# Tile 0's statistics shared between VectorE and ScalarE, first loads reordered, tile 2 normalised before its transposes, z sum moved to step 8

## The chip, the cores and the metric

The kernel runs on one core of one Trainium2 chip. The metric is the device time of one execution in microseconds. The kernel before took a median of 212.5 us in three runs (212.2, 212.5 and 212.92).

## What is computed

One input `x` (2048 rows of 512 columns, bf16) is normalised per row, and the result `xn` goes through two branches whose outputs are added to `x`:

```python
xn  = layernorm(x)                                   # mean and variance over 512, eps 1e-5
q, k, v = split(xn @ wqkv)                           # 32 heads of 16
pq, pk = phi(q), phi(k)                              # phi(t) = (t+1 if t>0 else exp(t)) + 1e-6
kv, z  = sum_s pk * v, sum_s pk                      # per head, over all rows
A = ((pq @ kv) / (pq . z + 1e-6)) @ wo               # linear attention
B = (silu(xn @ w_gate) * (xn @ w_up)) @ w_down       # 1792 wide
out = x + A + B
```

The outputs are in bf16.

## The kernel before, in words

The rows are cut into 16 tiles of 128. Everything stays in SBUF. The order of work on each engine is written out by hand: a small recorder (`K.op`, `K.dma`) appends each operation to the list of its engine and derives the semaphore waits from the named resources that it reads and writes. So each engine, and each of the two DMA queues (SP's and ACT's), works in exactly the order of the calls.

The program has three stages.

*Start (tiles 0 to 2).* TensorE runs filler matmuls on constants while the first tile of `x` is loaded. VectorE computes a tile's statistics (`bns` at line 291, `agg` at 294), then centres the tile without scaling it (`xc_half`, line 344, two halves of 256 columns). TensorE transposes the halves (`tp_first`, line 356), ScalarE copies them out of PSUM (line 365), and TensorE multiplies them with the key and query weights (`proj_first`, line 395). The row scale `rstd` is applied later, as the per-partition scale of the activations `first_ek`, `first_pk`, `first_eq`, `first_pq` (lines 452 to 470). `rstd_pow` (lines 312 and 319) computes `(var + eps)^-0.5` with an add (on VectorE for the tiles listed in `VD`, on POOL for the others) and a power on POOL.

*Steps (tiles 3 to 15).* VectorE writes the normalised tile `xn` (line 299), a DMA transpose on SP's queue writes `xnT` (line 372), TensorE computes keys and queries (`kproj`, `qproj`, line 381), ScalarE takes exponentials and a copy (lines 418 to 428), VectorE forms the features `pk` (`clip` at 435, `maxadd` at 444), and TensorE adds the outer product of `xn` and `pk` into four PSUM banks (`gtacc`, line 515: G = xn^T pk, from which `kv` is made later by one product with the value weights). POOL sums `pk` over the tiles into `zacc` (`zsum`, lines 503 and 507). One step is eight projection matmuls and four of `gtacc`. Tile t's projections use PSUM banks 2(t%2) and 2(t%2)+1; banks 4 to 7 hold `gtacc`'s sums, and earlier the start's transposes.

In the lists, step t computes the projections of tile t, while `STAT` names the tiles whose statistics are made in that step and `XN0`, `XN` those that are normalised and sent to the DMA transpose. Tiles 0 to 2 are transposed again by DMA (`transpose_dma` in steps 7 to 9), since their normalised form is needed by the last stage.

*Feed-forward stage.* From about 48 us, TensorE runs gate and up projections for 4 chunks of 512 rows x 14 column blocks (`ffn_mm`, line 679), and the output products of a finished chunk (lines 851 and 862) in between. Beside it, `z_split`, `z_cols`, `z_sum` and `z_rows` turn `zacc` into a row sum on every partition (two POOL copies, DMA transposes, a reduce on VectorE at line 734), and the queries' features are divided by their denominators (lines 809 to 833).

The weights are loaded over both queues: keys (`wk`, four chunks of 128 rows) and queries (`wq`) at the start, interleaved with tiles of `x`; the rest on SP's queue in step 10 and at the start of the last stage.

Of the kernel before, what the change touches and what calls it, by code (L numbers as in the profile page):

```python
# [7 lines left out]
ALU = mybir.AluOpType  # L8
# [100 lines left out]
def bass_parallel_sum__linear_attn_block__swiglu_ffn__prompt_kernel(  # L109
# [16 lines left out]
    with contextlib.ExitStack() as es:  # L126
        E = es.enter_context

        def sb(name, shape, d=bf):
            return E(nc.sbuf_tensor(name, [P] + shape, d))  # L130
# [19 lines left out]
        nb = sb("nb", [NT], f32)  # L150
# [44 lines left out]
        def xload(eng, h, t0, n, after=()):  # L195
            K.dma(
                eng, lambda: h.dma_start(x_sb[:, t0:t0 + n, :], xv[:, t0:t0 + n, :]),
                r=list(after), w=[("x", t0 + i) for i in range(n)],
            )
# [40 lines left out]
        xload("sp", sp, 0, 1)  # L240
        wqkv_load("act", act, "wk", 1, 0, 2)
        xload("sp", sp, 1, 1)
        wqkv_load("sp", sp, "wk", 1, 2, 1)
        wqkv_load("act", act, "wk", 1, 3, 1)
        xload("act", act, 2, 1)
        wqkv_load("sp", sp, "wq", 0, 0, 1)
        wqkv_load("act", act, "wq", 0, 1, 1)
        xload("sp", sp, 3, 1)
        wqkv_load("act", act, "wq", 0, 2, 1)
        wqkv_load("sp", sp, "wq", 0, 3, 1)  # L250
        xload("act", act, 5, 1)
        xload("sp", sp, 4, 1)
        xload("sp", sp, 6, 4, [("x", 3)])
# [52 lines left out]
        VD = (3, 5)  # L306
# [34 lines left out]
        def xc_half(t, h):  # L341
            K.op(
                "dve",
                lambda: dve.tensor_scalar(  # L344
                    out=xc_sb[:, t, h * HD:(h + 1) * HD], in0=x_sb[:, t, h * HD:(h + 1) * HD],
                    scalar1=mv[:, t, 0:1], scalar2=None, op0=ALU.subtract,
                ),
                r=[("x", t), ("mv", t)], w=[("xc", t, h)],
            )

        def tp_first(t, h, b):
# [11 lines left out]
            K.op(  # L363
                "act",
                lambda: act.activation(xcT[:, NDC * t + 2 * h:NDC * t + 2 * h + 2, :], tb, ACT.Copy),  # L365
                r=[bk(b)], w=[("xcT", t, h)],
            )
# [120 lines left out]
        def feat_k(t):  # L488
            e = t % NE
            clip(ek[:, e, :], ("ek", e))  # L490
            if t >= 3:
                zsum(t - 3, e)
            maxadd(pkq[:, t, 0, :], banks[kb(t)], ek[:, e, :], [bk(kb(t)), ("ek", e)], [("pk", t)])

# [29 lines left out]
        def stat(t):  # L524
            bns(t)
            agg(t)
            rstd_pow(t)

# [5 lines left out]
        bns(0)  # L534
        agg(0)
        rstd_pow(0)
        xc_half(0, 0)
        xc_half(0, 1)
        bns(1)
        agg(1)  # L540
        rstd_pow(1)
        xc_half(1, 0)
        xc_half(1, 1)
        bns(2)
        agg(2)
        rstd_pow(2)
        xn_dve(0)
        xc_half(2, 0)
        xc_half(2, 1)

        fill(8, 512)
        tp_first(0, 0, 4)
        fill(2, P)
        tp_first(0, 1, 5)
        fill(3, P)
        proj_first(0, "wk", 0)
        proj_first(0, "wk", 1)
        tp_first(1, 0, 6)
        tp_first(1, 1, 7)
        fill(4, P)  # L560
        first_ek(0)
        first_pk(0)
# [5 lines left out]
        tp_first(2, 0, 4)  # L568
        tp_first(2, 1, 5)
        proj_first(0, "wq", 1)  # L570
        proj_first(1, "wq", 1)
        clip(ek[:, 0, :], ("ek", 0))
        feat_pool(0)
        bns(3)
        agg(3)
        rstd_pow(3)
        bns(4)
        clip(ek[:, 1, :], ("ek", 1))
        first_pk(1)
        first_eq(0)  # L580
        first_pq(0)
        proj_first(2, "wk", 0)
        proj_first(2, "wk", 1)
        gtacc(0)
        xn_dve(2)
        xn(3)
        agg(4)
        first_feat(1)
        rstd_pow(4)
        xn_dve(1)  # L590
        first_ek(2)
        first_pk(2)
        first_eq(1)
        first_pq(1)
        clip(ek[:, 2, :], ("ek", 2))
        xn(4)
        proj_first(2, "wq", 0)
        proj_first(2, "wq", 1)
        gtacc(1)
        first_eq(2)  # L600
        xload("act", act, 14, 2)
        first_pq(2)
        first_feat(2)
        bns(5)
        agg(5)
        rstd_pow(5)
        gtacc(2)
        bns(6)
        agg(6)
        rstd_pow(6)  # L610
        xn(5)
        kproj(3)
        exp_k(3)
        qproj(3)
        exp_q(3)
        bns(7)
        clip(ek[:, 0, :], ("ek", 0))
        xn(6)
        agg(7)
        rstd_pow(7)  # L620
        zsum(0, 0)
        maxadd(pkq[:, 3, 0, :], banks[kb(3)], ek[:, 0, :], [bk(kb(3)), ("ek", 0)], [("pk", 3)])
        bns(8)
        xn(7)
        agg(8)
        rstd_pow(8)

        STAT = {4: (9,), 5: (10,), 6: (11,), 7: (12,), 8: (13, 14), 9: (15,)}
        XN0 = {5: (8,), 6: (9,), 7: (10,), 8: (11,), 9: (12, 13), 10: (14,)}
        XN1 = {}  # L630
        XN = {10: (15,)}

        for t in range(4, NT):
# [4 lines left out]
            for i in XN0.get(t, ()):  # L638
                xn(i)
            feat_k(t)  # L640
            for i in XN1.get(t, ()):
                xn(i)
            for i in STAT.get(t, ()):
                stat(i)
            for i in XN.get(t, ()):
                xn(i)
            if t in (7, 8, 9):
                transpose_dma(t - 7)
# [6 lines left out]
            if t == 12:  # L655
                masks()
# [4 lines left out]
        zsum(NT - 3, None)  # L661
        zsum(NT - 2, None)
        zsum(NT - 1, None)
# [236 lines left out]
        whalf("wu", wu_sb, B_w_up, 1)  # L900
# [58 lines left out]
```

## Time and profile before

| | |
|---|---|
| median of three runs | 212.5 us |
| profiled execution | 212.67 us, its span 211.3 us |
| TensorE matmul busy | 208.2 us (98%) |
| VectorE busy | 119.8 us (57%) |
| ScalarE busy | 69.9 us (33%) |
| POOL busy | 74.4 us (35%) |
| moved by DMA | 16.71 MB, mean 79 GB/s |
| granted TensorE clock, mean | 1.0 |

The span runs from the first to the last instruction of the profiled execution; the device time has 1.4 us around it. PE is TensorE, PEld its weight loads, DVE is VectorE, ACT is ScalarE, SP the engine that issues most DMAs. All times of single instructions below are microseconds from the span's start. A matmul on 512 columns is listed with some 0.38 us, because its record includes the pipeline's latency; what counts for throughput is the distance between two starts.

### The profile page before, as it was taken

The page shows a single profiled execution, that of the slowest core. Times are in us where ns is not written, and L with a number is a line of the kernel's source. Part 1 is how long each engine was busy: PE and PEld are TensorE (multiplying, and loading weights), DVE is VectorE, ACT ScalarE, POOL GpSimd, SP SyncE. Part 2 cuts the span into 40 slices and gives each one's busy share as a digit, 9 for nine tenths or more (in the row PEclk, how much of TensorE's full clock was granted, in tenths as well). Part 3 has the DMA queues.
Part 4 walks back from the last instruction along what each step waited for, and adds up shares of the span by engine and source line. Part 5 has one row for each costly group of instructions (what it writes and reads, how often), then busy time and mean ns, then how long its engine had stood idle before and what let it go on. Part 6 is the DMA issues. An engine that isn't in the chain of part 4 may idle for free.

```text
span 211.3 us, 2784 instructions
## 1 busy us (share of the span) xinstructions
PE 208.2 (98%) x995; PEld 96.3 (46%) x995; DVE 119.8 (57%) x245; ACT 69.9 (33%) x122; POOL 74.4 (35%) x95
## 2 busy tenths in 40 slices
PE   8999999999999999999999999999999999999996
PEld 3544444445444444444444444444444444444454
DVE  3899889434464775546274746364556535374121
ACT  3797666766543331213122312212032213121000
POOL 3637987749032444122140432130414032221100
DMA  5863344795694011110101010202021010110201
GB/s 187 281 177 75 54 99 88 197 374 190 165 363 96 0 25 25 50 28 25 50 2 50 19 33 26 50 0 50 3 50 25 25 25 29 48 28 25 51 28 50
DMA packets 29455, 16.71 MB, mean 79 GB/s; under 512 B 20224, under 2 KB 29056, under 8 KB 29440
## 3 DMA queue, kind: packets, MB, share of 16 engines
q1 hardware_dynamic: 28304, 15.34, 26.8%
q10 hardware_dynamic: 1136, 1.18, 1.8%
q8 instruction: 8, 0.13, 0.3%
q14 instruction: 7, 0.06, 0.1%
HBM read 9.70 MB, written 2.10 MB: 56 GB/s over the span
## 4 chain that ended last, share of the span: by engine, by line
PE 97%; DMA 1%; DVE 1%; ACT 0%; issue 0%
PE psum L679 46%; PE psum L862 23%; PE psum L381 11%; PE psum L515 7%; PE psum L851 7%; PE psum L395 3%; DMA x_sb<-in_A_x_dram 1%; PE psum L356 0%; PE psum L777 0%; PE psum L800 0%; DVE stats L291 0%; PE psum L263 0%; DVE out_sb L875 0%; ACT xcT L365 0%; DVE xc_sb L344 0%
## 5 line engine op out<-in xcount | busy, mean ns | idle before, releaser
L694 ACT ACTIVATE sg<-psum 128x512 bf16<-128x512 f32 x56 | 33.4, 598 | 106.8 <-PE psum L679 103.8
L679 PE MATMUL psum<-xnT,wg_sb 128*128 128x512 bf16 x224 | 57.5, 379 | 0.0
L679 PE MATMUL psum<-xnT,wu_sb 128*128 128x512 bf16 x224 | 57.5, 379 | 0.0
L809 POOL TENSOR_TENSOR prod<-pkq,zb 128x512 f32<-128x512 bf16 x16 | 18.6, 1163 | 57.5 <-DVE pkq L444 57.5
L679 PEld LDWEIGHTS psum<-xnT,wu_sb 128*128 128x128 bf16 x224 | 21.9, 98 | 26.4
L679 PEld LDWEIGHTS psum<-xnT,wg_sb 128*128 128x128 bf16 x224 | 21.9, 98 | 26.2
L875 DVE TENSOR_TENSOR out_sb<-psum,x_sb 128x512 bf16<-128x512 f32 (+1 forms) x17 | 11.2, 660 | 35.7 <-PE psum L862 35.7
L833 POOL TENSOR_TENSOR pqn<-pkq,rden 128x512 bf16<-128x512 bf16 x16 | 16.9, 1056 | 36.6 <-DVE rden L827 36.6
L700 DVE TENSOR_TENSOR pkq<-psum,sg 128x512 bf16<-128x512 f32 x28 | 19.2, 687 | 18.5 <-PE psum L679 14.0
L700 DVE TENSOR_TENSOR xn_sb<-psum,sg 128x512 bf16<-128x512 f32 x28 | 18.8, 671 | 14.4 <-PE psum L679 14.0
L862 PE MATMUL psum<-wd_sb,xn_sb 128*128 128x512 bf16 (+1 forms) x126 | 25.7, 355 | 0.0
L862 PE MATMUL psum<-wd_sb,pkq 128*128 128x512 bf16 x112 | 25.5, 379 | 0.0
L381 PE MATMUL psum<-wqkv_sb,xnT 128*128 128x512 bf16 x104 | 24.4, 379 | 0.0
L507 POOL TENSOR_TENSOR zacc<-zacc,pkq 128x512 f32<-128x512 f32 x15 | 17.3, 1157 | 4.9 <-DVE ek L435 4.5
L862 PEld LDWEIGHTS psum<-wd_sb,xn_sb 128*128 128x128 bf16 x126 | 12.3, 98 | 11.9
L862 PEld LDWEIGHTS psum<-wd_sb,pkq 128*128 128x128 bf16 x112 | 11.0, 98 | 13.2
L851 PE MATMUL psum<-m_sb,eq 128*128 128x512 bf16 (+1 forms) x68 | 16.6, 366 | 0.0
L515 PE MATMUL psum<-pkq,xn_sb 128*128 128x512 bf16 x64 | 16.0, 379 | 0.0
L381 PEld LDWEIGHTS psum<-wqkv_sb,xnT 128*128 128x128 bf16 x104 | 10.1, 98 | 12.6 <-DMA xnT<-xn_sb 0.5
L817 DVE TENSOR_REDUCE den<-prod 128x32 f32<-128x512 f32 x16 | 10.9, 684 | 5.9 <-POOL prod L809 5.9
L291 DVE BATCH_NORM_STATS2 stats<-x_sb 128x6 f32<-128x512 bf16 x16 | 10.9, 684 | 3.2 <-DMA x_sb<-in_A_x_dram 3.2
L444 DVE SCALAR_TENSOR_TENSOR pkq<-pkq,eq 128x512 bf16<-128x512 bf16 x16 | 11.1, 692 | 0.6
(59 smaller groups left out, 140.0 us busy)
## 6 DMA issues: line engine op xcount, KB each, us to landing
out_dram<-out_sb SPq DMA_DIRECT2D x15, 128.0 KB, 1.7
wg_sb<-in_B_w_gate_dram SPq DMA_DIRECT2D x2, 896.0 KB, 8.4
wu_sb<-in_B_w_up_dram SPq DMA_DIRECT2D x2, 896.0 KB, 6.2
wd_sb<-in_B_w_down_dram SPq DMA_DIRECT2D x1, 1792.0 KB, 10.1
x_sb<-in_A_x_dram SPq DMA_DIRECT2D x2, 512.0 KB, 4.0
x_sb<-in_A_x_dram SPq DMA_DIRECT2D x4, 128.0 KB, 4.1
wqkv_sb<-in_A_wqkv_dram SPq DMA_DIRECT2D x1, 512.0 KB, 9.3
wo_sb<-in_A_wo_dram SPq DMA_DIRECT2D x1, 512.0 KB, 10.2
```

Of the source, the lines that this page charges most:

```text
L381: (lambda c=c: pe.matmul(banks[b], xnT[:, c, t * P:(t + 1) * P], wqkv_sb[:, c, lo:lo + D], start=(c == 0), stop=(c == NDC - 1),))
L444: lambda: dve.scalar_tensor_tensor(out=dst, in0=src, scalar=0.0, in1=e, op0=ALU.max, op1=ALU.add,),
L507: lambda: pool.tensor_tensor(out=zacc[:, :], in0=zacc[:, :], in1=pk, op=ALU.add),
L515: (lambda c=c: pe.matmul(banks[4 + c], xn_sb[:, t, c * P:(c + 1) * P], pkq[:, t, 0, :], start=(t == 0), stop=(t == NT - 1),))
L679: (lambda c=c: pe.matmul(banks[b], w_sb[:, c, fc * P:(fc + 1) * P], xnT[:, c, C * 512:(C + 1) * 512], start=(c == 0), stop=(c == NDC - 1),))
L694: lambda: act.activation(sg[:, j % NSG, :], banks[gb], ACT.Silu),
L700: lambda: dve.tensor_tensor(out=hT(C, fc), in0=banks[ub], in1=sg[:, j % NSG, :], op=ALU.mult,),
L809: lambda: pool.tensor_tensor(out=p, in0=pkq[:, t, 1, :], in1=zb[:, :], op=ALU.mult),
L833: lambda: pool.tensor_tensor(out=pqn[:, t % NPN, :].rearrange("p (h e) -> p h e", e=DH), in0=pkq[:, t, 1, :].rearrange("p (h e) -> p h e", ...
L851: (lambda g=g: pe.matmul(dst, pqnT(t)[:, g, :], m_sb[:, g, lo:hi], start=(g == 0), stop=False,))
L862: (lambda fc=fc: pe.matmul(dst, hT(C, fc)[:, jj * P:(jj + 1) * P], wd_sb[:, fc, lo:hi], start=False, stop=(fc == NFC - 1),))
L875: lambda: dve.tensor_tensor(out=o, in0=src, in1=x_sb[:, t, lo:hi], op=ALU.add),
```

## The change

Tile 0: its mean is no longer taken from `bn_stats`. VectorE sums the first 256 columns and ScalarE the other 256, both scaled by -1/512 (`mean_dve`, `mean_act`), and the centring adds the two partial results. POOL adds them to one number `m0`, ScalarE takes the sum of (x + m0)^2 with a Square activation, and POOL makes variance, eps and power from it (`var_first`). `xn_first` normalises tile 0 with these.

Loads: tile 1 of `x` goes first on ACT's queue, ahead of the key weights; the third and fourth key chunk and all four query chunks go on SP's queue, as do tiles 3 to 5 of `x`; the load of tiles 14 and 15 is called during tile 0's projection instead of in the middle of tile 2's.

Tile 2: it is no longer centred and handled like tiles 0 and 1. VectorE normalises it, TensorE transposes it (`transpose_pe`) and ScalarE copies it into `xnT`; from there it is an ordinary tile, and it needs no DMA transpose later.

Order: tile 1's transposes stand between the halves of tile 0's projection; one wide filler matmul and the four narrow ones ahead of tile 1's projection are gone; `gtacc` of tiles 0 to 2 moves; tile 0's feature add moves from POOL to VectorE; the eps add of tiles 2, 4 and 6 to 8 moves from POOL to VectorE; in the steps, normalisation comes after `maxadd`. The z sum starts in step 8, with one tile a step, then two from step 11 on. The masks are made in step 7 instead of 12, and the second half of `w_up` is loaded in step 10 instead of behind the z transposes.

```diff
         xload("sp", sp, 0, 1)
+        xload("act", act, 1, 1)
+        wqkv_load("sp", sp, "wk", 1, 2, 1)
         wqkv_load("act", act, "wk", 1, 0, 2)
-        xload("sp", sp, 1, 1)
-        wqkv_load("sp", sp, "wk", 1, 2, 1)
-        wqkv_load("act", act, "wk", 1, 3, 1)
+        wqkv_load("sp", sp, "wk", 1, 3, 1)
         xload("act", act, 2, 1)
         wqkv_load("sp", sp, "wq", 0, 0, 1)
-        wqkv_load("act", act, "wq", 0, 1, 1)
+        wqkv_load("sp", sp, "wq", 0, 1, 1)
         xload("sp", sp, 3, 1)
-        wqkv_load("act", act, "wq", 0, 2, 1)
+        wqkv_load("sp", sp, "wq", 0, 2, 1)
         wqkv_load("sp", sp, "wq", 0, 3, 1)
-        xload("act", act, 5, 1)
         xload("sp", sp, 4, 1)
+        xload("sp", sp, 5, 1)
...
-        VD = (3, 5)
+        VD = (2, 3, 4, 5, 6, 7, 8)
...
+        def mean_dve():
+                lambda: dve.tensor_scalar(
+                    out=junk[:, 0:HD], in0=x_sb[:, 0, 0:HD], scalar1=-1.0 / D, scalar2=None,
+                    op0=ALU.mult, op1=ALU.add, accum_out=m1[:, :],
...
+        def mean_act():
+                    junk[:, HD:D], x_sb[:, 0, HD:D], ACT.Copy, scale=-1.0 / D, accum_out=m2[:, :],
...
+        def var_first():
+                "pool", lambda: pool.tensor_tensor(out=m0[:, :], in0=m1[:, :], in1=m2[:, :], op=ALU.add),
...
+                lambda: act.activation(junk[:, :], x_sb[:, 0, :], ACT.Square, bias=m0[:, :], accum_out=sq[:, :]),
...
+                    out=vpe[:, 0:1], in0=sq[:, :], scalar1=1.0 / D, scalar2=1e-5, op0=ALU.mult, op1=ALU.add,
...
+                lambda: pool.tensor_tensor(out=rstd[:, 0:1], in0=vpe[:, 0:1], in1=nhalf[:, :], op=ALU.pow),
...
+        def xn_first():
+                    out=xn_sb[:, 0, :], in0=x_sb[:, 0, :], scalar1=m0[:, :], scalar2=rstd[:, 0:1],
+                    op0=ALU.add, op1=ALU.mult,
...
         def xc_half(t, h):
+            if t == 0:
+                sc = dict(scalar1=m1[:, :], scalar2=m2[:, :], op0=ALU.add, op1=ALU.add)
...
-        bns(0)
-        agg(0)
-        rstd_pow(0)
+        mean_dve()
+        mean_act()
         xc_half(0, 0)
         xc_half(0, 1)
+        var_first()
         bns(1)
+        fill(7, 512)
+        tp_first(0, 0, 4)
+        fill(2, P)
+        tp_first(0, 1, 5)
+        fill(3, P)
         agg(1)
         rstd_pow(1)
         xc_half(1, 0)
         xc_half(1, 1)
+        proj_first(0, "wk", 0)
+        xload("act", act, 14, 2)
+        tp_first(1, 0, 6)
+        proj_first(0, "wk", 1)
+        tp_first(1, 1, 7)
+        first_ek(0)
+        first_pk(0)
         bns(2)
         agg(2)
         rstd_pow(2)
-        xn_dve(0)
-        xc_half(2, 0)
-        xc_half(2, 1)
-
-        fill(8, 512)
...
+        xn_first()
+        bns(3)
+        xn_dve(2)
+        agg(3)
+        clip(ek[:, 0, :], ("ek", 0))
+        rstd_pow(3)
+        first_feat(0)
+        xn(3)
         proj_first(1, "wk", 0)
         proj_first(1, "wk", 1)
         first_ek(1)
         proj_first(0, "wq", 0)
         proj_first(1, "wq", 0)
-        tp_first(2, 0, 4)
-        tp_first(2, 1, 5)
+        transpose_pe(2, 4)
         proj_first(0, "wq", 1)
         proj_first(1, "wq", 1)
...
+        kproj(2)
+        exp_k(2)
+        first_feat(1)
+        xn(4)
         gtacc(0)
...
+        qproj(2)
+        exp_q(2)
...
         gtacc(1)
...
+        kproj(3)
+        exp_k(3)
...
         qproj(3)
         exp_q(3)
+        gtacc(2)
...
-        STAT = {4: (9,), 5: (10,), 6: (11,), 7: (12,), 8: (13, 14), 9: (15,)}
-        XN0 = {5: (8,), 6: (9,), 7: (10,), 8: (11,), 9: (12, 13), 10: (14,)}
+        STAT = {4: (8,), 5: (9,), 6: (10, 11), 7: (12,), 8: (13, 14), 9: (15,)}
+        XN = {4: (7,), 5: (8,), 6: (9,), 7: (10, 11), 8: (12,), 9: (13, 14), 10: (15,)}
+
+        ZS = {8: (0,), 9: (1,), 10: (2,), 11: (3, 4), 12: (5, 6), 13: (7, 8), 14: (9, 10), 15: (11, 12)}
...
-            feat_k(t)
+            clip(ek[:, e, :], ("ek", e))
+            for i in XN.get(t, ()):
+                rstd_pow(i)
+            for i in ZS.get(t, ()):
+                zsum(i, e)
+            maxadd(pkq[:, t, 0, :], banks[kb(t)], ek[:, e, :], [bk(kb(t)), ("ek", e)], [("pk", t)])
+            st, no = STAT.get(t, ()), XN.get(t, ())
...
-            if t in (7, 8, 9):
-                transpose_dma(t - 7)
+            if t in (9, 10):
+                transpose_dma(t - 9)
...
+                whalf("wu", wu_sb, B_w_up, 1)
-            if t == 12:
+            if t == 7:
                 masks()
...
-        whalf("wu", wu_sb, B_w_up, 1)
```

## The prediction

> **What bounds the kernel now.** I read the page's busy shares and slices first, then the chain that ended last, then the timeline of the first 20 us, because only there does the chain leave TensorE. Busy shares, TensorE's slices and the chain's shares by engine:
>
> ```profile
> PE 208.2 (98%) x995; PEld 96.3 (46%) x995; DVE 119.8 (57%) x245; ACT 69.9 (33%) x122; POOL 74.4 (35%) x95
> PE   8999999999999999999999999999999999999996
> PE 97%; DMA 1%; DVE 1%; ACT 0%; issue 0%
> ```
>
> TensorE has no hole from the second slice on. So the kernel can gain only by starting TensorE's useful work earlier, or by closing small holes. The chain in order of time (start us, us, what):
>
> ```profile
> 0.80 2.37 DMA x_sb<-in_A_x_dram
> 3.20 0.70 DVE stats L291
> 3.93 0.19 DVE mv L294
> 4.15 0.30 DVE xc_sb L344
> 4.49 0.39 PE psum L356 x2
> ...
> 5.63 1.09 PE psum L395 x4
> 6.72 0.13 PE psum L356 x2
> ...
> 6.87 0.39 ACT xcT L365
> 7.26 0.05 issue
> 7.31 1.90 PE psum L395 x8
> ...
> 16.48 1.90 PE psum L381 x8
> 18.38 0.86 PE psum L515 x4
> ...
> 20.97 0.86 PE psum L515 x4
> ```
>
> From 18.38 each step of twelve 512-column matmuls takes 20.97 - 18.38 = 2.59 us, or 0.216 us a matmul, and so it stays to the end: nothing to win there. The window to judge is from the first useful matmul, which the timeline puts at 5.42 (I call this P0), to the first matmul of gtacc(3), there at 18.22. The work in it is 40 projection and 12 gtacc matmuls, 52 x 0.216 = 11.23, and eight transposes at 0.055, 0.44: 11.67 us. It took 12.80, so **1.13 us are lost**. By the timeline: 0.26 while matmuls still run at half rate (the first two issue 0.43 and 0.27 apart, so the rate doubled at about 5.96), 0.22 in four filler matmuls before 7.00, 0.31 waiting for xcT of tile 1 (7.00 to 7.31), 0.11 waiting at 13.6 for tile 2's features, 0.21 around 16.4 for tile 4's DMA transpose. The rows I price with (groups with shapes apart; count, busy us, mean ns, then idle):
>
> ```profile
> L365 ACT ACTIVATE xcT<-psum 128x256 bf16<-128x256 bf16 x6 | 2.1, 382 | 3.9 <-PE psum L356 3.8
> L452 ACT ACTIVATE ek<-psum,rstd 128x512 bf16<-128x512 f32 x3 | 2.1, 706 | 0.0
> L312 POOL TENSOR_SCALAR vpe<-mv 128x1 f32<-128x1 f32 x14 | 4.4, 314 | 6.8 <-DVE mv L294 6.8
> L319 POOL TENSOR_TENSOR rstd<-vpe,nhalf 128x1 f32<-128x1 f32 x16 | 9.7, 606 | 3.4 <-DVE vpe L312 2.3
> L344 DVE TENSOR_SCALAR xc_sb<-x_sb,mv 128x256 bf16<-128x256 bf16 x6 | 1.4, 282 | 0.1
> ```
>
> **Part 1: tile 0's statistics.** Removed from the path: bn_stats 0.70 and bn_aggr 0.19 plus gaps, 3.20 to 4.15. Added: two half-sums side by side. ScalarE's is a 256-wide copy: 0.38 by L365, from 3.22, so 3.60. VectorE's sums in one pass as bn_stats does (0.684 for 512 columns), estimated at 0.42 for 256, so 3.62. The centring starts at 3.66 instead of 4.15; tile 0's transposes at 4.00 instead of 4.49. But that is not yet P0, because **the Square stands ahead of the transposes' copies on ScalarE**. It needs m0, an add on POOL: 3.64 + 0.31 (L312, nearest in shape and weight) = 3.95; Square 4.00 + 0.71 (L452, same width, a per-partition operand) = 4.71; copy 4.75 + 0.38 + 0.06 to TensorE: P0 = 5.20, a gain of 0.22 where the centring gained 0.49. The sum operand of all three is in no row. Low end: no extra, Square at 0.60 (L694, no per-partition operand): P0 5.08. High end: the add at 0.61 (L319), Square at 0.73 (L464), and a separate read-out of 0.20 (a one-column ACTIVATE, L227) behind both ScalarE sums: P0 5.91. I take 5.20, the rows nearest in width and operands, and keep the ends. The Trainium skill speaks for the high end: "VectorE: DVE Perf Modes", in its section on two Vector instructions with no wait between them, counts an op that writes out its accumulator as two instructions; it gives no price, and no trace here shows one.
>
> rstd(0) comes from POOL at about 4.76 + 0.31 + 0.61 = 5.7, before exp needs it at 7.1: free. Its cover is tile 0's projection.
>
> **Part 2: the loads.** Before, by the trace's landings: x0 3.17, wk0-1 4.27, x1 4.63, wk3 4.99, wk2 5.34, x2 5.94, wq0 6.25, wq1 7.32, x3 7.50, wq2 8.03, wq3 8.20. A queue's n-th 128 KB lands at much the same time whatever it holds, so x1, first on ACT's queue, lands at about 3.7 (halfway to wk0-1's 4.27), wk0-1, now behind it, where wk3 did: 4.99. That is under P0 5.20. wk2 and wk3 take SP's places, 4.63 and 5.34, needed at 6.1. x2 keeps place and time. What moves from ACT's queue to SP's (wk3, wq1, wq2, x5) costs 0.43 us of issue each there; SP is done issuing at 5.2 and next waits for x3 anyway. x14-15 are now issued at about 5 instead of 12.93, so two more 128 KB units pass before x6 to x13. At 0.42 us a unit (3.17 to 8.79 for 13 units, 0.43) that is 0.84 later for what is behind.
>
> **Part 3: the order up to step 4.** With x1 at 3.7, bn_stats(1) starts after the centring at 4.17, where before it started at 4.66 (x1 landed at 4.63). From P0 on TensorE, still at half rate to 5.96: 5.20, 5.62, transposes(1,0) at 6.00, then two projections, transposes(1,1) 6.55. The copy starts 0.32 after its transposes (6.55 to 6.87 before): 6.32, done 6.70, tile 1's projection at 6.76 after a hole of 0.10; its second half at 7.31 after a hole of 0.12; end 7.74. Before, that point was 7.31 + 0.86 = 8.17. The fillers are gone.
>
> Tile 2 then goes through normalisation. VectorE by start-to-start times before: bn_stats(2) still at x2's landing, 5.98; aggr 6.70; vpe 6.91; xn(0) 6.99; bn_stats(3) 7.45 to 7.6 (x3); xn(2) 8.05, done 8.43. rstd(2) on POOL: 7.06 + 0.61, after tile 1's at 7.03. TensorE reaches its transposes at 7.74 + 0.86 = 8.60: free, by 0.1. wq(0,1) second half at 8.82, against wq3 at 8.2 to 9.0. The copy to xnT 9.03 + 0.60, kproj(2) 9.69, qproj(2) 11.45 (0.03 behind pq(0) on ScalarE, which runs on at 0.57 an instruction), gtacc(1) 12.3 (features at 11.87), kproj(3) at 13.2: tile 3's transpose is issued at 10.0 rather than 11.07 and took 2.5 us, 12.5, or some 13 behind the loads. xn(4) at 11.95 to 12.35, transpose landing at 14.9 to 15.8, kproj(4) at 15.77. gtacc(3) at 17.50. The losses left are 0.37 at half rate, 0.10, 0.12 and small ones. **Gain 18.22 - 17.50 = 0.72 us**, from the fillers, the wait for tile 1 and the one for tile 4's transpose.
>
> **Part 4: steps 4 to 15 and the z sum.** The same twelve matmuls a step. VectorE gets vpe of tiles 2, 4 and 6 to 8 (0.15 each); its work in seven steps is about 15 of 18.1 us. gtacc(t-1) has some 1.5 us of slack behind the clip. POOL is relieved until step 8, then adds one or two tiles (1.16 each) in 2.59. After step 15's clip five sums remain where four did: z_split ends near 53.4 instead of 53.07, its last transpose near 56, and VectorE reads it at 59.85: hidden by 3.8 us. The last half of wu, moved ahead, lands before wd; the first weights needed, wg at 48.4, landed at 43.18. Cost 0.
>
> **Sum.** The profiled execution took 212.67 (span 211.3); less 0.72 is 211.95. It stood 0.17 above the median of the runs, 212.5, so the median goes to **211.8**. With P0 at 5.08 the gain is 0.8, at 5.91 it is 0.36, since the first matmuls then run less of their time at half rate; if every loss closed, 1.13 + 0.34 = 1.5.
>
> **Rivals.**
>
> Square too long. P0 at 5.6 or later: gain 0.36 to 0.5, time 212.0 to 212.15. For: three unseen sums in a row, ScalarE in order. Against: the narrow rows above.
>
> The doubled rate comes later (the other side). Before, it came 5.1 us after the first filler, with one pause of 0.28 (fillers' last slot ends 4.21, transposes at 4.49). After, the eighth filler is missing: pauses 3.83 to 4.00 and about 4.95 to 5.20, and to 5.9 in the worst case. If pauses put the doubling off, each us at half rate costs 0.5 us: the gain is gone if it comes 1.44 us later (7.40), and if 5.1 us count anew from 4.00 it comes at 9.1 and costs 1.6: 213.4. Against: the pause before did no harm, and the sum of pauses grows little. The Trainium skill, "TensorE: Matmul & The Clock Gate", Part 1, has the clock judged in free-running windows of about 3.4 us that must be busy; a missed window would by it cost 1.7, 213.5. It adds in Part 4 that transposes do not count as busy in the same way, which would speak against this change.
>
> Loads late. wq2/wq3 by 0.84 (to 9.04, hole 0.2), or tile 3's transpose behind x6 to x13 (to 13.6, hole 0.4), or a new order on VectorE that makes xn(2) late: gain 0.1 to 0.5, or up to 0.5 lost if they add to late ScalarE sums: 212.0 to 213.0. For: slack of 0.1 in places. Against: DMA order has x3 early.
>
> **Numbers.** No change and a change under 0.3% (0.64 us) can't be told apart here. Forecast 0.60 (211.2 to 212.1; 0.48 of it past 0.64), Square too long 0.14, rate later 0.15, loads late 0.11 (half within the bound, the rest split). Faster 0.48 + 0.02 = 0.50; slower 0.15 + 0.04 = 0.19; same 0.31. The range for 8 in 10: 211.1, nearly all losses closed, to 213.0, where the missed rate begins.
>
> **What would show it.** Right: first useful matmul at 5.1 to 5.4, behind a copy that waits for the Square; no filler and no hole over 0.15 between tile 0's and tile 1's projections; gtacc(3) at about 17.5; every later start 0.7 earlier. Wrong: matmuls 0.43 apart beyond 6; read-out instructions on ScalarE; TensorE idle on DMA at 8.8 or 13.2, or on VectorE before transposes of tile 2; holes in steps 4 to 15.

## The result, and the profile after

The changed kernel took a median of 213.62 us (212.62 to 216.94 in 17 runs); the kernel before, beside it, 212.42 (211.99 to 212.97 in 17 runs). The ratio is 1.0056, with a 95% interval of 1.0040 to 1.0072. The change made the kernel slower by 0.56%, about 1.2 us, where 211.8 with an upper end of 213.0 was forecast. One of the 17, the 216.94, ran at a lower granted clock (0.992) and is left out of the ratio; the others took 212.62 to 214.64. The profiled execution took 213.24 us, its span 211.9.

The page of the changed kernel: busy shares, TensorE's slices, and the chain's shares by engine.

```profile
PE 207.2 (98%) x971; PEld 96.1 (45%) x990; DVE 119.4 (56%) x249; ACT 70.1 (33%) x124; POOL 71.6 (34%) x90
PE   6999999999999999999999999999999999999996
PE 96%; DMA 1%; issue 1%; DVE 0%; ACT 0%
```

TensorE still has no hole from the second slice on; only the first slice changed, from 8 tenths to 6. So what went wrong lies in the first few microseconds, and the chain in order of time shows it (start us, us, what):

```profile
0.79 3.00 DMA x_sb<-in_A_x_dram
...
3.81 0.52 ACT junk L358 x2
...
5.90 0.98 PE psum L456 x2
6.88 0.21 PE psum L417 x2
7.09 0.85 PE psum L456 x2
7.94 0.21 PE psum L417 x2
8.16 1.95 PE psum L456 x8
...
17.24 1.73 PE psum L442 x8
18.96 0.86 PE psum L569 x4
```

Two things are to be seen. The chain starts with tile 0's load, which ends at 3.79 and no longer at 3.17. And the first four projection matmuls (line 456) take 0.98 and 0.85 a pair: 0.43 to 0.49 a matmul, half rate, as long as the four run, while the eight from 8.16 on take 1.95, most of them at 0.216. Further down there is no wait of 0.1 or more. gtacc(3) stands at 18.96 where it stood at 18.38.

The rest of the span is the same for all kernels here: from gtacc(3) in the chain to the end it is 211.3 - 18.38 = 192.9 before and 211.9 - 18.96 = 192.9 after. With no later wait, **the span is the start of gtacc(3) plus 192.9**; I use this below to tell what the start costs from what is lost later. Two more profiled executions of the change have gtacc(3) at 19.41 and 19.18, one more of the kernel before has it at 18.07. In the one with 19.41 (213.94 us, slower than the median) TensorE waited not for tile 0 but for the first key weights, which now stand behind tile 1 on ACT's queue. Its chain starts with them:

```profile
1.34 4.85 DMA wqkv_sb<-in_A_wqkv_dram
...
6.33 1.01 PE psum L456 x2
```

They landed at 6.19 there, and at 5.23 and 5.16 in the other two profiles of the change.

The timeline of the changed kernel in its first profile (start us, us, engine, line, operation, tile and operand; in brackets the idle time before it and what ended it):

```profile
0.82 3.15 PE L267 MATMUL psum<-const-bfloat16-1.0 128*128 128x512 bf16 x7 [0.82 <-PEq L983]
...
3.81 0.42 ACT L358 ACTIVATE junk<-x_sb 128x256 bf16<-128x256 bf16 x1 [1.53 <-DMA x_sb<-in_A_x_dram]
...
4.13 0.19 ACT L358 ACTIVATION_READ_ACCUMULATOR junk<-x_sb 128x1 f32 x1
4.15 0.08 DVE L348 DVE_READ_ACCUMULATOR junk<-x_sb 128x1 f32 x1
...
4.40 0.19 POOL L366 TENSOR_TENSOR m<-m 128x1 f32<-128x1 f32 x1 [2.81 <-ACT junk L358]
4.71 0.72 ACT L371 ACTIVATE junk<-x_sb,m 128x512 bf16<-128x512 bf16 x1 [0.39 <-DVE xc_sb L406]
...
4.76 0.39 PE L417 MATMUL psum<-ident,xc_sb 128*128 128x128 bf16 x2 [0.79 <-DVE xc_sb L406]
...
5.43 0.36 ACT L426 ACTIVATE xcT<-psum 128x256 bf16<-128x256 bf16 x1
```

The fillers end at 3.97 and TensorE then waits 0.79 for the centred tile. The sums came near the prices forecast: 0.42 for each half-sum, 0.19 for the add on POOL (0.31 forecast), 0.72 for the Square, and two read-outs of 0.18 to 0.19 on ScalarE. P0, the first useful matmul, starts at 5.84.

So P0 is 0.64 later than forecast (5.84 against 5.20), and from P0 to gtacc(3) by the timeline it took 18.80 - 5.84 = 12.96, where 12.30 was forecast and the work at full rate is 11.67. Half rate to 8.49 costs (8.49 - 5.84) / 2 = 1.33, which is the whole of the 1.29 lost. The forecast had 0.37 for it.

### The profile page after: what moved, and what is told of

Its sections match the earlier page's. It is cut to its first block, busy times and chain, and to the rows that moved or that the text cites. A ratio compares the mean times of both kernels' runs of the same rounds, so it can differ in the third digit from the quotient of the medians.

```text
span 211.9 us, 2753 instructions
## 1 busy us (share of the span) xinstructions
PE 207.2 (98%) x971; PEld 96.1 (45%) x990; DVE 119.4 (56%) x249; ACT 70.1 (33%) x124; POOL 71.6 (34%) x90
## 4 chain that ended last, share of the span: by engine, by line
PE 96%; DMA 1%; issue 1%; DVE 0%; ACT 0%
PE psum L719 45%; PE psum L902 23%; PE psum L442 11%; PE psum L569 7%; PE psum L891 7%; PE psum L456 2%; DMA x_sb<-in_A_x_dram 1%; PE psum L417 0%; PE psum L817 0%; PE psum L840 0%; PE psum L267 0%; ACT junk L358 0%; DVE out_sb L915 0%; DVE xc_sb L406 0%; PE psum L332 0%
## 5 line engine op out<-in xcount | busy, mean ns | idle before, releaser
L442 PE MATMUL psum<-wqkv_sb,xnT 128*128 128x512 bf16 x109 | 26.1, 379 | 0.1
L442 PEld LDWEIGHTS psum<-wqkv_sb,xnT 128*128 128x128 bf16 x112 | 10.8, 98 | 13.4 <-ACT pkq L531 0.3
L323 POOL TENSOR_TENSOR rstd<-vpe,nhalf 128x1 f32<-128x1 f32 x15 | 9.1, 611 | 11.2 <-DVE vpe L316 10.6
```

Of the source, the lines that this page charges most:

```text
L442: (lambda c=c: pe.matmul(banks[b], xnT[:, c, t * P:(t + 1) * P], wqkv_sb[:, c, lo:lo + D], start=(c == 0), stop=(c == NDC - 1),))
```

## The experiments

The first theory has two parts. (a) Tile 0 lands late because tile 1, issued 0.13 us behind it on the other queue, shares its time. (b) With that and one filler less, TensorE pauses for 0.8 us (0.28 before) and its full rate comes 2.5 to 3 us later. The rivals: the sums on ScalarE and POOL are the loss; or the DMA transposes and the order on VectorE are, and would hold TensorE at the same place anyway.

### More fillers in the change, fewer in the kernel before

```diff
-        fill(7, 512)
+        fill(9, 512)
...
-        fill(3, P)
+        fill(4, P)
```

> The changed kernel with nine wide fillers instead of seven and four narrow ones instead of three behind the transposes of tile 0, so that TensorE has no pause over 0.15 before its first useful matmul at 5.84. Tile 0 still lands at 3.8. Theory B: the rate doubles at or before 6.2 in nearly all runs, the median falls by about 1.0 to 212.6 and the spread to about 1.0. Theory A alone: no change, 213.6. A third theory, that the doubling comes at a random phase whatever TensorE does before: no change, 213.6, with the same spread.

The changed kernel with two more wide fillers and one narrow one: 213.11 us (212.43 to 214.13, 12 runs), ratio to the kernel before 1.0026 [1.0009, 1.0044]. Full rate is there before P0. About half of the loss goes. Why not more, its chain shows:

```profile
9.02 1.07 POOL rstd L323
...
10.56 3.56 DMA xnT<-xn_sb
...
14.16 1.90 PE psum L442 x8
```

Tile 3's transpose took 3.56 and holds kproj(3) to 14.16; gtacc(3), at 18.65, is only 0.31 earlier than in the change.

```diff
-        fill(8, 512)
+        fill(5, 512)
```

> The kernel before with five wide fillers instead of eight: TensorE pauses from about 3.0 to 4.49 instead of from 4.2 to 4.49, and nothing else is changed; the first useful matmul stays at 5.42. Theory B: the doubling is put off in most runs, by up to 3.4, median 213.0 to 214.0 and a spread of 1.5 or more. Theory A alone, or a doubling at a phase that TensorE does not set: 212.4 as before.

The kernel before with three fillers less: 213.81 us (213.03 to 214.91, 8 runs), ratio 1.0059 [1.0038, 1.0081]. Nothing else is changed, tile 0 lands at 3.11, and the kernel is as slow as the changed one. Its chain:

```profile
5.57 1.71 PE psum L395 x4
7.27 0.43 PE psum L356 x4
...
8.12 2.01 PE psum L395 x8
...
13.93 3.46 DMA xnT<-xn_sb
...
17.45 1.90 PE psum L381 x8
19.34 0.86 PE psum L515 x4
```

The first four projections take 1.71, or 0.43 each, and the rate doubles at about 8.5, as in the change (8.49). That too few fillers alone can cost about 1 us (gtacc(3) at 19.34 instead of 18.38 or 18.07, the median up by 1.2) is thus shown.

### Tile 1's place in the load order

```diff
-        xload("act", act, 1, 1)
-        wqkv_load("sp", sp, "wk", 1, 2, 1)
+        xload("sp", sp, 1, 1)
         wqkv_load("act", act, "wk", 1, 0, 2)
+        wqkv_load("sp", sp, "wk", 1, 2, 1)
```

> The changed kernel with tile 1 of x moved back to second place on SP's queue, behind tile 0, and the first key weights first on ACT's queue; all else as changed. Theory A (the late landing of tile 0, 3.78 against 3.17, is what costs): tile 0 lands at 3.2, the first useful matmul moves from 5.84 to about 5.3, and the median falls by some 0.5 from 213.6 to 213.1 or less. Theory B (TensorE's rate doubles late, 8.49 against 5.96 in the profiled runs, because its fillers leave pauses): tile 0 lands early too, but the pauses stay about as long in sum, doubling stays late in many runs, the median stays above 212.9 and the runs spread by 1.5 to 2. If A were all of it, the median would be at or below 212.4.

The changed kernel with tile 1 back on SP's queue: tile 0 lands at 3.41, the pause is 0.4, full rate is there by 4.4, and yet it took 214.32 us (213.54 to 216.09, 6 runs), ratio 1.0082 [1.005, 1.0113]. The start up to the first matmul was mended and the kernel was slower. Its chain says where most of it went:

```profile
10.12 4.64 DMA xnT<-xn_sb
...
14.80 1.90 PE psum L442 x8
...
23.71 4.67 DMA xnT<-xn_sb
...
28.51 1.89 PE psum L442 x8
...
47.52 1.28 DVE ek L496
```

Tile 3's transpose was issued 0.7 earlier than in the change and landed 1.4 later (14.76 against 13.39). A second one, tile 8's, took 4.67 and put kproj(8) back by 0.75. A clip of 1.28 (line 496) put gtacc(15) back by 0.34; the section on the z sum comes back to such clips. And ahead of all that, not in the chain, TensorE sat idle 0.83 us for a chunk of the query weights:

```profile
9.74 1.04 PE L456 MATMUL psum<-wqkv_sb,xcT 128*128 128x512 bf16 x4 [0.83 <-DMA wqkv_sb<-in_A_wqkv_dram]
```

```diff
+        xload("act", act, 1, 1)
         wqkv_load("act", act, "wk", 1, 0, 2)
-        xload("sp", sp, 1, 1)
```

> The kernel before with one edit: tile 1 of x goes first on ACT's queue, ahead of the first key weights, instead of second on SP's. Theory A: tile 0 lands near 3.8, the whole start is 0.6 later, median 212.4 + 0.6 = 213.0. Theory B adds to it: the wide fillers still end at 4.2, so TensorE pauses for some 0.9 instead of 0.28 before the first transposes, and the doubling comes later in part of the runs: 213.0 to 213.8 and a wider spread than the 1.0 of before. If tile 0 lands at 3.2, both are wrong on the cause of its lateness.

The kernel before with only this of the change: 213.71 us (212.91 to 214.7, 12 runs), ratio 1.0043 [1.0017, 1.0069]. Its chain:

```profile
0.81 3.37 DMA x_sb<-in_A_x_dram
...
18.83 0.86 PE psum L515 x4
```

Tile 0 lands at 4.18, 0.85 to 1.2 later than in the six profiles of kernels with the old order of the first loads (3.00 to 3.33), though its own load is issued at the same moment. That tile 1's place delays tile 0 is shown: wherever tile 1 goes first on ACT's queue, tile 0 lands at 3.68 to 4.18 (eight profiles), and with tile 1 on SP's queue at 3.00 to 3.41 (twelve).

That the two only share the time isn't shown, and two things speak against it. With tile 1 on SP's queue a load stands beside tile 0 just as well: the first key weights, 256 KB, issued on ACT's queue at the same 0.13 us behind it. And from 3.0 to 3.6 us the DMA engines moved less in all: 133 to 188 GB/s in the eight profiles, 277 to 379 in the twelve (133 in the change's first profile, 311 in that of the kernel before), though further loads had been issued on both queues. So tile 1's load beside tile 0's slows both queues, and why stays open. The Trainium skill, "DMA: Bandwidth & Descriptors", section "Issuing engines are not separate DMA queues", says that transfers started by different engines run on the same 16 DMA engines and interleave. The trace of the change agrees in that packets of both queues moved between 2.4 and 2.8 us; the rate that fell isn't explained by it.

In this kernel TensorE paused 1.31 us behind its eight wide fillers (4.18 to 5.49) and yet had its full rate at 5.5. So here the late landing alone costs: gtacc(3) at 18.83 instead of 18.38 or 18.07. The twelve runs fall into six of 212.91 to 213.28, the profiled one among them, and six of 214.13 to 214.7, of which there is no trace.

### The loads behind the transposes

In the changed kernel, as in the one before, SP's queue holds 1 MB of x (tiles 6 to 13) ahead of tile 3's transpose, which the change issues earlier. Does the transpose wait for these loads?

```diff
-        xload("sp", sp, 10, 4)
...
-        xload("act", act, 14, 2)
...
         xn(4)
+        xload("sp", sp, 10, 4)
...
         exp_q(3)
+        xload("act", act, 14, 2)
```

> The changed kernel with two loads issued later: tiles 10 to 13 of x behind tile 4's DMA transpose on SP's queue instead of ahead of tile 3's, tiles 14 and 15 behind tile 3's exponentials. Theory T (tile 3's transpose stands in SP's queue behind the loads and lands 0.6 after the last of them, at 13.4 to 14.8 in the profiles so far, though it is issued at 10.1 to 10.8): it lands at about 13.1, and in executions where TensorE's rate doubles early the projection of tile 3 no longer waits; where it doubles at 8.5 TensorE arrives at 14.5 and nothing is gained. Median 213.2, against 213.6 for the changed kernel. Without T: 213.6.

> Both edits: loads behind the transposes, and nine wide and four narrow fillers. If the late doubling and the queue are the two causes and each hides the other, this gains more than the two alone together: 212.4 (more fill alone gave 213.1). If T is wrong: 213.1. In its profile the projection of tile 3 follows the outer product of tile 1 without a hole.

> Loads behind the transposes, tile 1 of x back in second place on SP's queue, eight wide and four narrow fillers. Tile 0 lands at 3.2 to 3.4, the first useful matmul starts at about 5.4, and all that is left of the change works as it was forecast: 211.9, 0.5 below the kernel before. If tile 0's landing does not matter behind VectorE's chain, which hangs on tile 2's landing: 212.4 as for the run with both edits.

The three have these loads moved (the one of tiles 14 and 15 from tile 0's projection); the second has also nine wide fillers, the third eight and tile 1 on SP's queue, and both have four narrow ones. Ratios: 1.0100 [1.0077, 1.0122], 1.0051 [1.0039, 1.0063] and 1.0033 [1.0021, 1.0045] (5 or 6 runs each, medians 215.15, 213.84, 213.44). Tile 3's transpose now takes 2.5 us however early it is issued (10.28 to 12.79 in the third). But the loads now stand beside tile 5's. The chain of the second:

```profile
16.28 3.77 DMA xnT<-xn_sb
...
20.19 1.89 PE psum L441 x8
```

The obstacle was moved by two tiles, not taken away: tile 5's transpose took 5.94, 3.77 and 3.63. It landed just after the last of the loads then in flight (22.09 after 22.01, 20.06 after 19.46, 19.41 after 18.81). The same holds for tile 3's in the kernels with the loads ahead of it: 14.11 after 13.49 with more fillers, 14.76 after 14.15 with tile 1 on SP's queue. So the answer is yes: such a transpose lands behind the loads in flight. Of the fillers, the difference of the first two shows once more what they are worth here: 1.3 us.

In a fourth, the third kernel (but with three narrow fillers instead of four) has the Square and what follows it on POOL (the new `var_rest`; only the add stays in `var_first`) placed behind tile 0's copies:

```diff
         var_first()
...
         tp_first(0, 1, 5)
+        var_rest()
```

> As the run before, with the Square of tile 0 put behind tile 0's two copies on ScalarE instead of ahead of them, and three narrow fillers instead of four. The copies no longer wait for it: first useful matmul at about 5.2 instead of 5.4. But the row scale of tile 0 comes at about 7.2, when its exponential needs it at 7.1 and VectorE at 7.0. Median 211.8 if the Square was what the first matmul waited for, 211.9 to 212.1 if the row scale becomes the next wait.

Ratio 1.0066 [1.0054, 1.0078], against 1.0033 without it: worse by 0.7 us, though P0 came at 5.09 instead of 5.45. Its chain:

```profile
6.46 0.55 POOL rstd L384
...
7.41 1.09 POOL rstd L322 x2
...
8.53 0.41 DVE xn_sb L302
```

Tile 0's power on POOL now ends at 7.01. POOL works in the order of its list, so the powers of tiles 1 and 2 come behind it and end at 8.50, and VectorE's normalisation waits for them. So the Square ahead of the copies, one of the rivals, was the better place.

### The order on VectorE, and all of it together

POOL's power took 1.06 instead of 0.55 us where a two-input add on VectorE had begun just before it, and VectorE's normalisation waited for it. In the timeline of the changed kernel:

```profile
12.11 1.06 POOL L323 TENSOR_TENSOR rstd<-vpe,nhalf 128x1 f32<-128x1 f32 x1 [1.94 <-DVE vpe L316]
...
13.21 0.41 DVE L303 TENSOR_SCALAR xn_sb<-x_sb,mv,rstd 128x512 bf16<-128x512 bf16 x1 [0.44 <-POOL rstd L323]
```

The next kernel is the change with nine wide fillers and the one-input statistics in that place, the add behind the normalisation:

```diff
+        bns(4)
-        first_feat(0)
         xn(3)
+        first_feat(0)
...
-        bns(4)
...
+        bns(5)
-        first_feat(1)
         xn(4)
+        first_feat(1)
...
-        bns(5)
```

> The changed kernel with nine wide and four narrow fillers and a new order on VectorE alone: the statistics of tiles 4 and 5 stand ahead of the normalisation of tiles 3 and 4, and the feature adds of tiles 0 and 1 behind them. Theory V (POOL's power takes 1.06 instead of 0.55 beside the two-input feature add, and VectorE waits 0.45 for it twice, so the transposes of tiles 3 to 5 go out late): both powers take 0.55 to 0.6, VectorE does not wait for them, tile 4's transpose is issued 0.8 earlier than with more fill alone (13.39), tile 5's as well (16.04). Median 212.7 against 213.1, or 212.9 if tile 3's transpose still waits behind the loads. Without V: 213.1.

It took 212.84 us (212.55 to 214.0, 12 runs), ratio 1.0008 [0.9988, 1.0028]: a difference from the kernel before can no longer be measured. The powers took 0.56, and tile 4's transpose was issued at 12.20, where the kernel with more fillers alone had 13.39. Tile 3's, now issued earliest of all with the loads ahead of it, took longest. The profiled execution, at 213.83, is among the longest of the twelve; its chain:

```profile
8.85 0.56 POOL rstd L323
...
9.87 5.15 DMA xnT<-xn_sb
...
15.06 1.90 PE psum L442 x8
```

The last step adds to this what the others showed: tile 1 on SP's queue, eight wide fillers, the load of tiles 10 to 13 behind tile 6's transpose, and that of tiles 14 and 15 on SP's queue at the end of step 4.

> The same order on VectorE, tile 1 of x back in second place on SP's queue, eight wide and four narrow fillers, the loads of tiles 10 to 13 behind tile 6's transpose and of tiles 14 and 15 behind step 4. If tile 0's landing, the pauses, the queue and VectorE's order are all that went wrong, the start works as forecast: outer product of tile 3 at 17.5 to 17.9 instead of 18.22 before, median 212.0 to 212.2 against 212.5. If something else binds the transposes (they then take over 3 us from issue to landing though no load stands ahead of them), it stays at 212.8 or above.

It took 213.01 us (212.39 to 213.89, 12 runs), ratio 1.0011 [0.9989, 1.0033]. In the profiled execution, its fastest, the start comes out nearly as the prediction had it: P0 at 5.12 (5.20 forecast), gtacc(3) in the timeline at 17.70 (17.50 forecast). The chain there:

```profile
17.87 0.86 PE psum L568 x4
...
45.34 1.27 DVE ek L495
...
47.39 1.04 PE psum L568 x4
```

gtacc(3) at 17.87, 0.5 earlier than in the first profile of the kernel before and 0.2 earlier than in the second. Yet the span, 211.2, is not 210.8 but 0.4 longer: gtacc(15) waits for a clip of 1.27 at 45.34, where the clip took 0.29 in the change. A second profiled execution of the same kernel (213.46 us) had gtacc(3) at 18.10, since its rate doubled only at 6.8 (3.6 in the first), and lost 1.1 later, 0.34 of it at gtacc(15) again. Its chain:

```profile
22.51 4.65 DMA xnT<-xn_sb
...
27.30 1.89 PE psum L441 x8
```

Tile 8's transpose took 4.65 and put kproj(8) back by 0.73. The same is in one of the other two profiles of the change (23.82, 4.27 long; 0.36 lost). In the first profile of the kernel before it took 4.89, and nobody waited: issued at 21.27, it landed at 26.16, and kproj(8) came at 27.0. In the changed kernel it is issued at 23.38 to 23.82, 2.1 us or more later. Normalisation now stands behind maxadd and the tiles are spread differently over the steps; that this is why it is issued later was not tried by itself.

### The z sum

```diff
-        ZS = {8: (0,), 9: (1,), 10: (2,), 11: (3, 4), 12: (5, 6), 13: (7, 8), 14: (9, 10), 15: (11, 12)}
+        ZS = {4: (0, 1)}
+        ZS.update({t: (t - 3,) for t in range(5, NT)})
```

> The run with all mended, with the z sum one tile a step again (tiles 0 and 1 in step 4, then one tile a step). In that run's profile the outer product of tile 3 came 0.51 earlier than before, but the last stage only 0.18 earlier: from step 12 on VectorE's clip took 1.1 to 1.3 instead of 0.29 beside POOL's two adds a step, and the outer product of tile 15 waited. Theory Z (the two adds a step hold the clip): clips at 0.3 in steps 12 to 15, no wait ahead of the outer product of tile 15, last stage 0.5 earlier than before, median 212.6 against 213.0. Without Z: 213.0.

> The kernel before with the z sum alone moved as in the change (from step 8, two tiles a step from step 11). Forecast of the record: no cost, 212.5. Theory Z: clips of 0.6 to 1.2 in steps 12 to 15 and a wait of 0.1 to 0.4 ahead of the outer product of tile 15: 212.6 to 212.9.

The mended kernel with the old z sum: 213.67 us (213.39 to 213.91, 12 runs), ratio 1.0037 [1.0019, 1.0054]. Its time doesn't tell about z, because `wu` landed at 50.43 and held the last stage, but its profile does: the last three clips took 0.29, and gtacc(15) didn't wait. The kernel before with the new z sum: 212.49 (211.91 to 213.26, 12 runs), ratio 0.9979 [0.9954, 1.0003], which leaves no loss and no clear gain. Its clips of steps 12 to 15 took 1.12, 1.35, 0.72 and 0.65, and yet gtacc(15) didn't wait.

So the new z sum makes clips long wherever they begin well inside one of POOL's adds: with one exception (0.29) such a clip ended 0.15 us after the add. In the three profiles of the change the clips began in the last 0.08 us of an add, and took 0.29. In five profiles of kernels made from it (tile 1 on SP's queue, the third and fourth of the moved loads, the mended kernel twice) they began inside one, and gtacc(15) came 0.33 to 0.34 later.

### What holds the kernel before

In the five profiles of the kernel before, and of those made from it, that have the load of tiles 14 and 15 in its old place, tile 4's transpose took 3.3 to 3.6 us, and TensorE waited 0.1 to 0.4 for it. That load was issued 0.07 to 0.14 us ahead of the transpose, on the other queue. Two kernels differ from the one before in nothing but the place of that load: behind tile 7's transpose on SP's queue, or during tile 0's projection.

```diff
         first_eq(2)
-        xload("act", act, 14, 2)
...
+            if t == 4:
+                xload("sp", sp, 14, 2)
             if t in (7, 8, 9):
```

```diff
         proj_first(0, "wk", 0)
+        xload("act", act, 14, 2)
         proj_first(0, "wk", 1)
...
         first_eq(2)
-        xload("act", act, 14, 2)
```

> The kernel before with one thing moved: the load of tiles 14 and 15 is issued on SP's queue at the end of step 4, behind the transposes up to tile 7's, and no longer on ACT's queue at about 12.9. Theory: in the kernel before, tile 4's DMA transpose (issued 12.5 to 13.0, landing 16.1 to 16.4, so 3.4 to 3.6 us) is slow because that load runs beside it, and it holds the projection of tile 4 by about 0.2 us. Then the transpose takes about 2.5 us here (landing 15.0 to 15.6), the pause of 0.2 ahead of that projection goes, gtacc(3) starts at 17.8 to 18.1 where it started at 18.1 to 18.4, and the median falls by 0.2 to 0.3, to a ratio of about 0.999. Rival: the load itself is not the cause, and the transpose still takes 3.4 us or more; or the load now slows tile 8's transpose, which was the next, to 5 us and more, and the projection of tile 8 waits: ratio 1.000 to 1.004.

> The kernel before with the load of tiles 14 and 15 called during tile 0's projection, as in the change (issued at about 5 and not at 12.9). Theory: it is through before tile 4's transpose is issued, which then takes about 2.5 us; but 0.25 MB more pass ahead of tiles 6 to 13, so these land some 0.8 later and tile 3's transpose (issued 10.6 to 11.1, 2.5 to 3.2 us) lands at 13.6 to 14.2 where kproj(3) wants it at 14.1 to 14.5: no gain or loss past 0.2, ratio 0.998 to 1.002. If tile 3's transpose takes 3.5 us or more, as where it came in early in earlier runs, kproj(3) waits and the ratio is 1.002 to 1.004.

The transpose took 2.44 us in both (12.92 to 15.36 and 12.81 to 15.24), so the load was its cause, and TensorE has no pause left there. The chain of the first:

```profile
13.55 1.04 PE psum L515 x4
14.59 3.45 PE psum L381 x16
18.04 0.86 PE psum L515 x4
```

The sixteen projection matmuls of tiles 3 and 4 follow each other at 3.45 / 16 = 0.216. But the times are 212.26 and 212.24 us beside 212.30: ratios 0.9993 [0.9983, 1.0003] and 0.9998 [0.9987, 1.0008]. gtacc(3) at 18.04 is no earlier than the 18.07 of the second profile of the kernel before. So in the first, with this wait gone, the next one, TensorE waiting for tile 2's features ahead of 13.55, stands at almost the same time. No version was found that is clearly faster than the kernel before.

Of four runs I used only the profiles, as further executions of the same kernels: two of the change (213.94 and 213.36 us), one of the mended kernel and one of the kernel before (212.26).

## Why the prediction was wrong, point by point

| step | forecast | measured |
|---|---|---|
| Part 2, tile 0 lands | 3.17, as before | 3.78 (3.70, 3.73 in two more profiles) |
| Part 1, from that landing to P0 | 2.03 | 2.06 |
| P0 | 5.20 | 5.84 (6.33, 5.79) |
| full rate from | 5.96 | 8.49 (about 8.5 and 9.0 in two more) |
| lost to half rate after P0 | 0.37 | 1.33 |
| other losses from P0 to gtacc(3) | 0.26 | none |
| gtacc(3), timeline | 17.50 | 18.80 |

The first failure is in **Part 2**. It moved tile 1 to the head of ACT's queue and priced when tile 1 would land; it left tile 0's landing as it was. The rule used, that a queue's n-th load lands at the same time whatever it holds, says nothing of what two queues do to each other. It held to 0.3 us for the loads that follow in the first profile, but not for tile 0's and tile 1's. This costs 0.6 us. The key weights, put behind tile 1, landed at 5.23, 5.16 and 6.19 where 4.99 was forecast; in the third profile TensorE waited 0.51 for them, and P0 came at 6.33.

The larger failure is **Part 3's half rate to 5.96**. The time at which the rate doubles was taken from one profile of the kernel before and kept, though a filler was taken away. The rival "the doubled rate comes later" is what came, and nearly at its price: 1.6 and 213.4 us for a doubling at 9.1, where 8.49 cost 0.96 more than forecast and the profiled execution took 213.24. It was given 0.15, on the ground that the pauses grow little; with tile 0 late the pause was 0.79, not 0.17. The kernel before with fewer fillers shows the late rate alone, the change with more fillers shows it undone. The rival's mechanism, that pauses put the doubling off, is shown in part only: a pause of 1.31 behind eight fillers did no harm, and seven fillers with a pause of 0.42 had the full rate by 4.4. What seven fillers with a short pause do in most executions is open. Part 3's other half was right: the fillers' place, the wait for tile 1 and the one at tile 4's transpose are gone.

**Part 1** was right in its sum, though partly by luck, since two errors cancel: the add on POOL was cheaper (0.19, not 0.31), and the read-outs came on top. The high end of 5.91 spoke of read-outs, as the Trainium skill does for VectorE ("VectorE: DVE Perf Modes", in its section on two Vector instructions with no wait between them). The trace agrees that they are instructions of their own, but the high end was not needed. "Square too long" fell: the 0.64 by which P0 is late is the landing.

The third failure is **Part 3's landing of tile 3's transpose**, 12.5, or 13 behind the loads; the runs with the change's loads show 13.39 to 15.02. In the change itself it cost nothing, since it landed at 13.39 and TensorE came to kproj(3) only at 14.65. But the forecast hung on it all the same: the kernel with tile 1 on SP's queue had tile 0 at 3.41 and the full rate by 4.4, and yet took 214.32, with the query chunk at 9.69 (9.04 in the rival **"loads late"**) and this transpose at 14.76. So that rival is true behind the first loss, and this is why mending the fillers brought 0.5 and not 1.2 us.

**Part 4's "cost 0"** failed for the transposes of tiles 7 and 8 in the longer executions: I counted VectorE's work in the steps, and not by how much less cover the later issue leaves. For the z sum it held in the change and in the kernel before, where no wait came of it, though `z_split` ended at 55.96 and not at 53.4; in the mended kernel it cost 0.33 at gtacc(15). And **the gain of 0.72 from the start itself** was reachable only in part: 0.51 between the first profiles of the mended kernel and of the kernel before, none between the second ones (18.10 and 18.07). In the median it did not show at all.

What stays open: why tile 1's load disturbs tile 0's; why one to three of the transposes issued between 19.5 and 29 us take 2.8 to 4.9 us in every profile; and why the loads ahead of tile 3's transpose land later in some kernels (the last at 12.35 to 12.75 in the change, at 13.49, 14.15 and 14.31 in three made from it). The change's median also lies 0.4 us above its first profile; the one slower profile shows waits for the key weights and for tile 8's transpose, and the other runs have no trace.

## What to carry to other kernels

When a change takes a filler away or moves the first real work later, look in the profile when the rate doubles, and do not take that time over from the old kernel: here eight or nine wide fillers were enough to double it by 6.9 us in every profile, and five or seven mostly were not. A load moved up beside the critical one may delay it: price the critical load again, and not only the one that was moved; here the key weights in that place did no harm and the next tile of `x` did. And a gain at the start lasts only if every later transfer still has cover: look for the next wait behind the one that you remove, here a transpose behind loads in flight, before you count the gain.

## What the runs showed of the hardware

- **The rate of TensorE.** With eight or nine wide fillers (3.4 us of busy time and up) the rate doubled between 3.5 and 6.9 us in all fourteen profiles, also with a pause of 1.31 behind them, and without any pause at 3.6 in one and at 6.8 in the other profile of one kernel. With seven or five, and a pause behind them of 0.69 to 1.29, it doubled between 8.5 and 10.0 in five profiles; with seven and a pause of 0.42 by 4.4 in one. The Trainium skill, "TensorE: Matmul & The Clock Gate", Part 1, has a free-running window of about 3.4 us; a group that comes so much later agrees with a missed window, and no run shows the window itself.
- **Which load stands beside a load matters.** Tile 0 of `x` (128 KB) lands at 3.00 to 3.41 with 256 KB of key weights issued 0.13 us behind it on the other queue, and at 3.68 to 4.18 with tile 1 of `x` there; the DMA engines then move 133 to 188 GB/s from 3.0 to 3.6 us instead of 277 to 379.
- **A DMA transpose of a 128x512 tile** takes 2.4 to 2.6 us alone in most cases. Beside a load of 256 KB issued 0.07 to 0.14 us ahead of it on the other queue it took 3.3 to 3.6, and landed 0.54 to 0.56 after that load, in five profiles. Behind 1 MB of loads on its own queue it took 2.5 to 5.2; where it took 3.1 or more (five profiles, among them 10.56: 3.56, 10.12: 4.64, 9.87: 5.15, by time of issue) it landed 0.6 to 0.7 after the last of them. In the last three it is issued earlier than in the change and lands later; the loads land later too, and why they do is open.
- **POOL and VectorE beside each other.** A power on one column on POOL takes 0.55 us, also where a two-input add on VectorE begins during it, and 1.06 where that add began 0.04 us before it. The other way round, VectorE's clip of 512 columns takes 0.29 us, and 0.51 to 1.35 where it begins with 0.36 us or more left of one of POOL's adds of the z sum. The kernel before with nothing but the z sum moved shows it (0.65 to 1.35 in steps 12 to 15).
- **The read-out of a sum** is an instruction of its own: 0.18 to 0.19 us on ScalarE, 0.08 on VectorE.
